# GpSimd's casts, squares and gathers wait for the VectorE instruction ahead of them, in a new order of all queues

## The chip, the cores and the metric

One Trainium2 chip, one of its cores. The metric is the time of one execution on the device in microseconds (us); the time of a kernel is the median of its runs.

## The reference

Block-sparse attention, and on its result a feed-forward network (FFN) with a squared relu:

```python
# q, k, v: (4, 8, 768, 64) f32; blocks of 32 rows, 24 of them; sampled_blocks: (24, 3)
scores = q @ k.T / 8
mask   = |blk_i - blk_j| <= 1  or blk_i in (0, 23)  or blk_j in (0, 23)  or blk_j in sampled_blocks[blk_i]
attn   = softmax(where(mask, scores, -1e9))
x      = (attn @ v), heads side by side           # 3072 x 512
out    = relu(x @ w_in) ** 2 @ w_out              # 512 -> 2048 -> 512
```

## The kernel before

Work is cut into tasks of a few instructions each. A task is a Python function with the things it waits for and the buffers that it takes and frees. One string, `PROGRAM`, lists all tasks in the order in which they are emitted: a word `V48` is task 48 on VectorE (DVE), `P` is TensorE (PE), `A` ScalarE (ACT), `G` GpSimd (POOL), `S` SyncE (SP, the queue of most DMAs), and `/2` says which of the four PSUM tiles `X` the task takes. Each engine executes its own words in order and waits by semaphores only for what a task depends on. So the string sets both the order on each queue and, for work that several engines can do, the engine.

A unit `u` is two heads of one batch (16 units, 4 per batch). Loads bring q, k, v in f32; `cast_qk` and `cast_v` turn them into bf16 (in `qc` and `VB`) on DVE, POOL or ACT; q and k are transposed into `QKT` on PE (batch 0, `transp`, `evac`) or by a DMA of SP (`transp_dma`).

Batches 0 and 1 are done densely, 256 queries at a time: `scores` on PE, `exps` on ACT (line 360, into a `pT` buffer), `masks` on DVE (line 367: `pT` times a mask tile that lies in a `VG` buffer), `values` on PE, `normalize` on DVE (lines 410 and 413), and a transposition into the FFN's input `xT`.

Batches 2 and 3 are done in six visits `v` of 128 queries (two groups `g` of two blocks). For a group only the needed keys and values are brought together: `k_gather` (lines 593 to 599) copies keys from `QKT` to a `KG` buffer with block numbers from registers, on POOL or DVE. `v_gather` brings rows of V from a copy in HBM to a `VG` buffer, either by one indirect DMA from POOL (line 579) or by six DMAs from SP with block numbers from registers (line 582); `v_window` brings the rows that need no number (lines 552, 556). Then `s_scores`, `s_exps` (623), `s_masks` on DVE (630), `s_values` (653), `s_normalize` on DVE (659, 662, into `XS`) and `s_transp`, a transposing DMA of SP from `XS` into `xT` (666). The registers are filled by `load_blocks` (TENSOR_LOAD, line 561) from the table `tab`.

The FFN takes tiles of 256 rows: `hidden` on PE (four parts for each of four units of 512 hidden columns), `relu` on ACT (707) or DVE (709), `square` on ACT (718), POOL or DVE (720), `output` on PE, `out_copy` on ACT or DVE (121, 123), `store`. `w_load` brings the weights in eight parts on POOL's queue. Line 203 is the helper `pair`, which issues nearly all matmuls; 121 and 123 are the helper `copy`.

Of the kernel before, what the change touches and what calls it, by code (L numbers as in the profile page):

```python
# [17 lines left out]
AOP = mybir.AluOpType  # L18

P = 128  # L20
# [5 lines left out]
def kernel(  # L26
# [92 lines left out]
    def copy(e, out, in_):  # L119
        if e == "ACT":  # L120
            A.copy(out=out, in_=in_)
        else:
            (V if e == "DVE" else G).tensor_copy(out=out, in_=in_)  # L123
# [239 lines left out]
    def masks(a, e):  # L363
        u, q0, w, cs = a
        pT = ptile[a].rearrange("p h (c q) -> p h c q", q=w)
        m = MK[q0][:, cs[0]:cs[-1] + 1]
        V.tensor_tensor(out=pT, in0=pT, in1=m[:, None].broadcast_to([P, 2, len(cs), w]), op=AOP.mult)  # L367
# [216 lines left out]
    def k_gather(b, v, g, e):  # L584
# [8 lines left out]
        eng.tensor_copy(out=to[:, :, 0], in_=src[:, :, :, 2 * w * (g - 1):2 * w * (g + 1)])  # L593
        if there.get((n, g % 2)) != b:
            there[n, g % 2] = b
            eng.tensor_copy(out=rows[:, :, :, RS * w:(RS + 1) * w], in_=src[:, :, :, 0:w])
            eng.tensor_copy(out=rows[:, :, :, (RS + 1) * w:], in_=src[:, :, :, (nb - 1) * w:nb * w])
        for r_ in range(RS):
            eng.tensor_copy(out=rows[:, :, :, r_ * w:(r_ + 1) * w], in_=src[:, :, :, bass.ds(at[r_] * w, w)])  # L599
# [26 lines left out]
    def s_masks(u, v, gs, e):  # L626
# [3 lines left out]
        V.tensor_tensor(out=pT, in0=pT, in1=m[:, None].broadcast_to([P, 2, n]), op=AOP.mult)  # L630
# [82 lines left out]
    def square(T, f, i, n, e):  # L713
# [5 lines left out]
        else:  # L719
            (G if e == "POOL" else V).tensor_mul(out=g, in0=r, in1=r)  # L720
# [217 lines left out]
    tb["slots"] = T_(table_slots, deps=[t, p], get=tmp)  # L938
    hb = Buf("X")
# [26 lines left out]
    for T in TILES:  # L966
# [3 lines left out]
        for f in range(0, NF, n_u):  # L970
# [4 lines left out]
            for part in range(parts):  # L975
# [4 lines left out]
                             put=[xb[b, c0]] if f + n_u == NF and end else []))  # L980
# [21 lines left out]
        A29 G35 P4/3 V32 P30/0 P12/2 P14/3 P9/1 P5/1 V31 P33/1 V111 P36/3 P0/2 A37 V1 V34 P102/2 V209 V46 P47/0 P106/1 A103 V48 P104/3  # L1002
        V43 A107 P44/0 G57 P7/2 V45 A105 P58/1 V54 P113/0 V59 P55/2 A114 P117/3 G41 V56 P2/1 V67 A118 P115/2 V3 P108/0 A116 V64 P127/1
        V109 P10/3 P65/3 A128 P123/2 V66 A124 P68/1 P125/3 G75 V69 V63 P92/1 P110 A126 P133/2 G76 V112 A134 P137/3 G52 S28 S42 S18 S19
        V93 S20 P88/0 A138 G38 V155 V89 P84/1 P119/2 G74 V85 A60 P86/0 P39/3 P135/1 V120 G73 A87 V40 A136 P121 P61/0 G49 P129/3 V122
        V62 G77 V70 P176/2 P170/0 P139/1 A177 G81 V130 G80 A171 V140 P146/2 P131 V132 A147 P149/3 V172 P71/0 P141 V142 A150 V72 P50/2
        P173/1 V148 P781/0 A174 P782 V178 P189/3 P783 V51 A190 V175 P90/1 P15/2 P96/2 P784 V91 A97 P183/3 V151 A785 P94/2 P179/1 V95
        A184 G787 P143/0 P774/2 V180 P775 A144 V191 G78 P186/3 P181 P776 V182 A187 P777 V145 P157/0 V778 A786 P152/3 A158 P160/1 V188
        P788/2 A161 V153 P163/0 P789 V185 A164 P790 V162 P154 P217/1 P791 A156 V159 A218 P192/0 V165 P795/3 A792 V193 S82 P166/1 S83
        V296 V219 S53 S254 A779 G794 S253 P194 P100/2 A780 P796 V195 V167 A101 P214/0 P797 G793 A215 P168 P798 V169 P211/2 V799 P824/1  # L1010
        G79 A212 P825 P196/0 G256 V216 P826 A197 P199/3 P818/2 G801 S257 P827 A200 P819 V828 P202/0 A800 S261 P228/3 P820 G22 A203
        S262 P821 V213 P812/1 S269 A229 V822 P813 G258 P220/0 A829 P814 V201 P245/2 S259 P221 A246 V198 P815 P802/3 V222 A816 P231/2
        V266 P223 P803 A232 V204 S267 P239/1 V230 P804 A224 A240 V264 S270 P242/0 P205/2 V233 S265 A243 P225/1 P206 P805 V207 A226
        S277 V274 P288/0 S436 S255 P208 P806 V227 A289 S275 V247 P11/1 P291/1 A823 P234/0 V241 P807 A292 V210 V244 P98/2 P235 V272
        P808 A99 V236 A817 S273 P298/2 V290 P248/1 P237 A299 P809 V238 S278 V293 P285/0 S279 V300 P249 A810 P830/2 V250 P831 A286 V282
        P304/3 P251 P832 V260 A305 P301/0 V252 P833 S263 V287 P852/1 A302 S334 S283 V834 P853 P846/3 G280 P313/0 V303 P854 A314 P316/2
        S281 P855 P847 A317 V856 G284 P294/0 P848 A835 S271 P295 V306 P310/1 S21 P849 G268 V297 A311 P864/2 V318 P865 S440 A850 P307/0
        V315 P866 S438 A857 P308 G851 S446 P355/3 P867 V309 A356 P322/1 V868 P858/0 P859 A323 P349/3 V357 P325/2 P860 A350 V312 P861
        P836/1 V276 A326 V351 S456 P319/3 A862 P328/2 V327 S439 P320 S447 A329 V321 P352/0 P837 S811 V324 A353 S454 P339/2 V330 P838
        A340 V354 P331/3 P342/0 A869 S385 V341 P332 P358/2 V333 P839 A343 V23 S335 G441 P359 A863 P336/3 P361/0 G443 P840 A337 P841  # L1020
        G451 A362 S622 P364/3 G449 P842 A365 P373/0 G445 S450 P843 A374 G461 P870/3 A844 S444 P367/0 V338 P871 A368 V344 S463 P872
        V347 V360 S455 V366 S442 P376/0 P345/1 A377 V363 P379/2 P346 P873 S452 V348 A380 V369 P403/0 P874 A404 V375 S464 P370/2 V378
        P400/1 P393/0 V381 P371 A401 P875 V372 S471 S448 A394 V402 P382/1 P390/2 V405 P383 A391 P387/0 P876 V384 A388 V395 S386 P406/1
        P886/2 V392 A407 P887 V457 P427/0 P877 A428 V465 P24/1 P888 S497 S462 A878 G453 P889 V408 S458 P880/0 A890 P881 P430/3 S466
        P882 V27 G891 A431 P883 P409/2 A884 P926/3 V26 P927 A885 P410 G469 P415/0 V398 V25 P928 V411 G467 A416 P892/1 S608 V389 P424/2
        S879 P893 A425 P929 S468 V432 P894 A930 P895 V426 P396/0 S470 A896 P16/2 V429 P898/3 S845 P397 S616 A931 P418/2 P433/1 V399
        P899 V459 A419 P932/0 P933 V474 S460 P412/2 P900 A413 P901 V417 P934 A902 S473 P434 V420 P935 V435 P482/3 G903 P904/2 A483
        V936 A897 P492/1 P905 V414 A493 P914/3 G503 P915 P480/0 S499 S623 P421/1 A481 P916 S542 P422 P906 G472 V423 V484 P907 S437
        G937 P917 P487/1 P908 V918 A488 P477/1 P490/0 P909 G501 A478 V504 A491 P485/1 P920/3 A919 G543 V494 P921 V479 V621 P475/0 P910
        A486 G500 V489 V625 A476 P911 V613 P495/1 A912 G546 S632 S913 V547 P511/2 S607 P505/0 V496 P922 A512 S520 S502 P923 A506  # L1030
        P954/1 V924 G627 P955 P514/2 P508/0 P956 A515 V507 G524 P557/3 S545 P957 V513 A509 P948/2 A925 P949 S614 P938/0 G544 A558 S498
        P939 V516 A958 V525 P551/3 S523 P950 A552 P940 V510 P554/3 P951 A555 P548/1 P941 G589 S628 A549 P517/3 A952 P966/1 G959 V518
        A953 P967 P535/2 P942 V550 S519 A536 P529/3 P943 G521 S626 V559 P526/2 P944 V590 G522 A527 P945 V537 P968 V609 A946 P960/2
        P961 V556 A530 P969 V528 P532/0 P962 A970 S540 S615 V553 P963 S585 G586 S624 P988/3 A971 V964 P989 P560/1 A533 V531 P990 A965
        V534 P594/2 P994/0 V561 A595 P995 P991 G567 S562 P996 A992 P538/1 V619 V568 S631 A993 P597/3 P972/2 S606 V539 A598 P997 V596
        S541 P600/1 P973 A601 G587 P1000/3 A998 V617 S620 P974 G999 P975 S610 P572/1 P1001 A573 S630 P982/0 G637 P1002 S588 P1003
        P575/1 P983 V1004 A576 P976 V611 P984 P578/1 P569/3 P985 V629 S612 A570 P977 V599 A986 V633 P978 S563 G565 S618 A579 V602
        P1034/3 A1005 P591/0 G635 V574 S634 P979 A592 P1035 G564 S638 P1028/1 A980 V593 P1036 S566 V580 P1029 A987 P1037 P1030 S639
# [50 lines left out]
```

## Time and profile before

| | before |
|---|---|
| times of 3 runs | 257.20, 259.04, 257.91 us |
| median | 257.91 us |
| the profiled execution | 258.88 us |
| its span in the profile | 257.10 us |
| granted TensorE clock | 1.00 |
| PE, DVE, ACT, POOL busy | 243.1, 171.3, 183.6, 98.8 us |

The span goes from the first to the last recorded instruction or transfer; 1.78 us of the profiled execution lie outside it. Busy times are sums over one engine, and PEld (weight loads) overlaps PE. In the lines of the trace, `X<-xT,w_in_sb` reads: output X, inputs xT and w_in_sb; what stands in brackets behind a line is the time that the engine stood idle before it and what ended that wait.

### The profile page before, as it was taken

To read this page: it belongs to the slowest core of one execution; us is meant where nothing else is said; L and a number is where in the kernel's file an instruction comes from. 1 tells how busy PE (TensorE), PEld (TensorE's weight loads), DVE (VectorE), ACT (ScalarE), POOL (GpSimd) and SP (SyncE) were. 2 spreads that over 40 slices of the span, in tenths; PEclk is the share of its full clock that TensorE was granted. 3 is DMA by queue.
4 is the path that set the end of the run, shared out by engine and by line. 5 is a ranking of instruction groups with operands and counts; after the bars stand their busy time and mean duration, and the time that the engine had idled before them with its cause. 6 is when DMAs were issued, how large, how long until landed. Compare 5 with 4: busy or idle time off the path is not lost.

```text
span 257.1 us, 12061 instructions
## 1 busy us (share of the span) xinstructions
PE 243.1 (95%) x5265; PEld 182.1 (71%) x5265; DVE 171.3 (67%) x408; ACT 183.6 (71%) x217; POOL 98.8 (38%) x178
## 2 busy tenths in 40 slices
PE   7888999999999997998998999999999999999993
PEld 4667879678874677975864867866875677767683
DVE  7778988899889995969916756657536725730301
ACT  3899999998999797846783975675965286623640
POOL 3183247003316026198556314264357620412100
PEclk9999999999999999999999999999999999999999
DMA  6999989999999996999699779998474923044022
GB/s 200 374 250 207 206 205 155 270 202 252 250 281 179 197 202 153 340 229 154 188 243 202 194 174 167 251 214 199 129 206 95 189 40 60 5 121 148 23 86 83
DMA packets 64692, 47.08 MB, mean 183 GB/s; under 512 B 31567, under 2 KB 60624, under 8 KB 64640
## 3 DMA queue, kind: packets, MB, share of 16 engines
q1 hardware_dynamic: 58512, 37.82, 64.7%
q0 software_dynamic: 5440, 8.05, 16.8%
q8 instruction: 41, 0.67, 1.1%
q10 hardware_dynamic: 688, 0.46, 0.6%
q14 instruction: 11, 0.09, 0.1%
HBM read 35.51 MB, written 7.91 MB: 169 GB/s over the span
## 4 chain that ended last, share of the span: by engine, by line
PE 53%; DVE 5%; DVEq 1%; issue 1%; ACT 1%; ACTq 0%
PE X L203 49%; PE X L653 4%; DVE VB L123 1%; ACT pT L623 1%; DVEq L561 1%; DVE MKS L123 1%; DVE pT L630 1%; DVE r L709 0%; DVE KG L599 0%; DVE qc L123 0%; DVE XS L413 0%; DVE KG L593 0%; DVE XS L662 0%; DVEq L599 0%; DVE rs L410 0%
## 5 line engine op out<-in xcount | busy, mean ns | idle before, releaser
L203 PE MATMUL X<-xT,w_in_sb 64*128 64x256 bf16 x1536 | 100.8, 269 | 2.8 <-issue 1.5
L203 PE MATMUL X<-w_out_sb,g 64*128 64x512 bf16 (+3 forms) x960 | 95.2, 334 | 0.1
L203 PEld LDWEIGHTS <-w_in_sb 64*128 64x128 bf16 x1536 | 74.6, 94 | 16.0 <-issue 5.4
L360 ACT ACTIVATE pT<-X 128x1024 bf16<-128x1024 f32 x72 | 70.6, 1030 | 7.6 <-PE X L203 6.8
L623 ACT ACTIVATE pT<-X 128x768 bf16<-128x768 f32 (+1 forms) x56 | 41.6, 766 | 26.5 <-PE X L203 23.9
L203 PEld LDWEIGHTS <-g 64*128 64x128 bf16 x960 | 40.3, 94 | 26.3 <-PE X L203 0.4
L720 POOL TENSOR_TENSOR g<-r 128x1024 bf16<-128x1024 f32 (+1 forms) x20 | 31.6, 1587 | 64.4 <-ACT r L707 47.2
L707 ACT ACTIVATE r<-X 128x1024 f32<-128x1024 f32 x28 | 29.8, 1068 | 20.6 <-PE X L203 20.5
L709 DVE TENSOR_SCALAR r<-X 128x1024 f32<-128x1024 f32 x20 | 24.5, 1224 | 26.7 <-PE X L203 13.7
L367 DVE TENSOR_TENSOR pT<-pT,VG 128x1024 bf16<-128x1024 bf16 x60 | 40.9, 715 | 0.2
L718 ACT ACTIVATE g<-r 128x1024 bf16<-128x1024 f32 (+1 forms) x40 | 35.2, 899 | 2.7 <-DVE r L709 2.5
L203 PE MATMUL X<-QKT 64*128 64x256 bf16 (+1 forms) x384 | 31.6, 250 | 3.3 <-DVE XS L413 1.3
L630 DVE TENSOR_TENSOR pT<-pT,MKS 128x768 bf16<-128x768 bf16 (+1 forms) x48 | 27.6, 607 | 10.7 <-ACT pT L623 10.5
L203 PEld LDWEIGHTS <-QKT 64*128 64x128 bf16 x384 | 16.7, 95 | 9.5 <-issue 4.1
L579 POOL DMA_INDIRECT VG<-rows,idx x19 | 20.2, 1061 | 4.4 <-issue 2.6
L203 PEld LDWEIGHTS <-pT 64*128 64x128 bf16 x768 | 16.0, 94 | 1.9
L203 PE MATMUL X<-VB,pT 64*128 64x65 bf16 x768 | 17.1, 190 | 0.0
L203 PEld LDWEIGHTS <-KG 64*128 64x128 bf16 x528 | 13.8, 95 | 4.5 <-issue 0.2
L659 DVE RECIPROCAL ss<-X 128x8 f32<-128x8 f32 x12 | 2.5, 206 | 19.5 <-PE X L653 17.3
L653 PEld LDWEIGHTS <-pT 128*64 128x64 bf16 x624 | 11.9, 111 | 4.9 <-issue 3.7
L203 PE MATMUL X<-QKT,KG 64*128 64x64 bf16 x528 | 15.3, 190 | 0.1
L123 POOL CAST VB<-vs 128x768 bf16<-128x768 f32 x9 | 7.8, 869 | 16.5 <-DMA vs<-in_v_dram 16.4
(107 smaller groups left out, 210.3 us busy)
## 6 DMA issues: line engine op xcount, KB each, us to landing
vs<-in_v_dram SPq DMA_DIRECT2D x14, 384.0 KB
ks<-in_k_dram SPq DMA_DIRECT2D x13, 384.0 KB
qs<-in_q_dram SPq DMA_DIRECT2D x12, 384.0 KB
out_dram<-ys SPq DMA_DIRECT2D x9, 512.0 KB
VG<-rows SPq DMA_DIRECT2D x20, 132.0 KB
w_in_sb<-in_moe_w_in_dram POOLq DMA_DIRECT2D x4, 512.0 KB, 8.6
w_out_sb<-in_moe_w_out_dram POOLq DMA_DIRECT2D x4, 512.0 KB, 9.9
rows<-VB SPq DMA_DIRECT2D x2, 792.0 KB
```

Source lines behind the costliest of these rows:

```text
L123: (V if e == "DVE" else G).tensor_copy(out=out, in_=in_)
L203: last = nc.tensor.matmul(out(r ^ crossed), lhsT(r ^ crossed, rows), rhs(r ^ crossed, rows), skip_group_check=True, **kw)
L360: A.activation(out=pT[:, :, 0:n], in_=stile.pop(a)[:, :, 0:n], func=AF.Exp, scale=scale)
L367: V.tensor_tensor(out=pT, in0=pT, in1=m[:, None].broadcast_to([P, 2, len(cs), w]), op=AOP.mult)
L579: G.indirect_dma_start(out=to[0:RS * HB], out_offset=None, in_=pairs, in_offset=bass.IndirectOffsetOnAxis(ap=idx[0:RS * HB, g - 1:g], axis=0))
L623: A.activation(out=pT[:, :, 0:n], in_=stile.pop((u, v, gs))[:, :, 0:n], func=AF.Exp, scale=scale)
L630: V.tensor_tensor(out=pT, in0=pT, in1=m[:, None].broadcast_to([P, 2, n]), op=AOP.mult)
L653: nc.tensor.matmul(po[i * D:(i + 1) * D, h, a * VW:(a + 1) * VW], pts[g][:, h, c * D:(c + 1) * D], val, start=a == 0 and c == 0, stop=c == ...
L707: A.activation(out=to, in_=src, func=AF.Relu)
L709: V.tensor_scalar(out=to, in0=src, scalar1=0.0, scalar2=None, op0=AOP.max)
L718: A.activation(out=g, in_=r, func=AF.Square)
L720: (G if e == "POOL" else V).tensor_mul(out=g, in0=r, in1=r)
```

## The change

It has four parts.

1. A new helper, `through_port`, is put around the masks (`masks`, `s_masks`), the casts of q, k and v, the copies of `k_gather` and the squares. On DVE it remembers the instruction. On POOL it makes the instruction wait for the one of DVE that was remembered last, if no other POOL instruction has waited for it yet. DVE does not wait for POOL in return. 39 tasks of POOL carry such a wait in the new order.
2. `load_blocks` is no longer a part of `table_rows`. It becomes six tasks of its own: for POOL, DVE and SP, one for the groups below 4 and one for the others.
3. The last part of `hidden` of each unit, not only of the tile's last unit, counts as a user of the `xT` buffer, so that units may come in any order.
4. `PROGRAM` is new: another order on all queues, and other engines for some tasks. DVE has fewer casts (11 fewer of 128x384 keys, for instance), three more output copies (2 to 5) and two more relus (20 to 22). ACT has three fewer output copies (9 to 6), two fewer relus, and three more half squares (15 to 18). POOL has more casts, 6 instead of 9 half squares, and 11 instead of 19 indirect gathers. The eight others are six DMAs each on SP: its `v_gather` DMAs go from 18 to 66. The number of matmuls, 5265, stays.

```diff
     def copy(e, out, in_):
         if e == "ACT":
-            A.copy(out=out, in_=in_)
-        else:
-            (V if e == "DVE" else G).tensor_copy(out=out, in_=in_)
+            return A.copy(out=out, in_=in_)
+        return (V if e == "DVE" else G).tensor_copy(out=out, in_=in_)
+
+    before_port = []
+
+    def through_port(e, made):
+        if e == "DVE":
+            before_port[:] = [made.ins]
+        elif e == "POOL" and before_port:
+            tc.add_manual_dep(made.ins, before_port.pop().name, SYNC, reason="the port that both read through")
...
-        copy(e, VB[b % 2][:, :, 2 * a:2 * a + 2, 0:D].rearrange("p n t d -> p t n d"), raw[u][2])
+        through_port(e, copy(e, VB[b % 2][:, :, 2 * a:2 * a + 2, 0:D].rearrange("p n t d -> p t n d"), raw[u][2]))
...
-        V.tensor_tensor(out=pT, in0=pT, in1=m[:, None].broadcast_to([P, 2, n]), op=AOP.mult)
+        through_port(e, V.tensor_tensor(out=pT, in0=pT, in1=m[:, None].broadcast_to([P, 2, n]), op=AOP.mult))
...
-            (G if e == "POOL" else V).tensor_mul(out=g, in0=r, in1=r)
+            through_port(e, (G if e == "POOL" else V).tensor_mul(out=g, in0=r, in1=r))
...
     def table_rows(e):
         V.tensor_scalar(out=idx, in0=low[1][:, P:P + GR], scalar1=float(HB), scalar2=lane, op0=AOP.mult, op1=AOP.add)
-        load_blocks("POOL")
-        load_blocks("DVE")
-        load_blocks("SP")
...
-    def load_blocks(e):
-        for g in wanted[e]:
+    def load_blocks(g0, g1, e):
+        for g in [g_ for g_ in wanted[e] if g0 <= g_ < g1]:
...
+    for e_ in ("POOL", "DVE", "SP"):
+        T_(load_blocks, 0, 4, deps=[tb["slots"]])
+        T_(load_blocks, 4, nb, deps=[tb["slots"]])
...
-                             put=[xb[b, c0]] if f + n_u == NF and end else []))
+                             put=[xb[b, c0]] if end else []))
...
-        A29 G35 P4/3 V32 P30/0 P12/2 P14/3 P9/1 P5/1 V31 P33/1 V111 P36/3 P0/2 A37 V1 V34 P102/2 V209 V46 P47/0 P106/1 A103 V48 P104/3
+        P0/0 P17/1 A35 A302 V117 A18 A38 G41 P36/2 V1 P2/3 S161 P39/1 G52 G60 P14/0 G63 G47 P34 V3 P92/3 P42/0 A37 P94/2 A93 V40 G58
```

In the new kernel the lines stand some four to seven further down: the masks at 374 and 634, the gathers of V at 583 and 586, the squares at 724.

POOL's queue before, at the middle of the program (batch 2's first visits). `L579` are indirect gathers of V, `L720` is a square; the brackets name the semaphores that an instruction waits for.

```order
L579 DMA VG_207<-rows_70,idx 96x1056 [waits DMAHW5_49,DMASW0_49,DVE_49]
L720 TENSOR_TENSOR g_99<-r_82 128x1024 [waits DVE_49]
L579 DMA VG_208<-rows_70,idx 96x1056 [waits DMASW1_49]
L579 DMA VG_209<-rows_70,idx 96x1056 [waits DMASW2_49]
L579 DMA VG_208<-rows_70,idx 96x1056 [waits DMASW3_49,DVE_49]
L593 COPY KG_118<-QKT 128x4x64 [waits PE_49]
```

And in the new order, at the same visits:

```order
L583 DMA VG_208<-rows_70,idx 96x1056 [waits DMASW2_49]
L122 CAST VB_191<-vs_79 128x2x6x64 [waits DVE_49]
L122 CAST qc_106<-ks_77 128x384 [waits DMAHW0_49,DMAHW3_49,DVE_49,Pool_49]
L122 CAST qc_106<-ks_77 128x384 [waits Pool_49]
L724 TENSOR_TENSOR g_100<-r_83 128x1024 [waits Activation_49]
L724 TENSOR_TENSOR g_101<-r_81 128x1024 [waits DVE_49,Activation_49]
L597 COPY KG_119<-QKT 128x4x64 [waits PE_49,Pool_49]
```

Casts for batch 3 stand here now in place of gathers; the casts and the second square wait for DVE.

DVE's queue before, where the tables for the visits are finished, among the last masks of batch 1. `MKS` are the masks of the visits, `idx` the rows that the indirect gathers take.

```order
L367 TENSOR_TENSOR pT_87<-pT_87,VG_208 128x1024
L123 CAST MKS<-X_147 128x5x64 x3
L123 CAST MKS<-X_147 128x6x64 x3
L524 TENSOR_SCALAR idx<-X_147,lane 128x11
L561 TENSOR_LOAD tab x6
L410 RECIPROCAL rs<-X_148 128x4
L413 TENSOR_TENSOR XS<-X_148,rs 128x2x2x64
```

The new order has the loads at two places, ahead of the first gather of keys on DVE and, further down, ahead of the division of batch 2's first visit (`ss`):

```order
L417 RECIPROCAL rs<-X_147 128x4
L420 TENSOR_TENSOR XS<-X_147,rs 128x2x2x64
L565 TENSOR_LOAD tab x2
L597 COPY KG_118<-QKT 128x4x64
...
L634 TENSOR_TENSOR pT_87<-pT_87,MKS 128x2x192
L565 TENSOR_LOAD tab x4
L663 RECIPROCAL ss<-X_148 128x8
L666 TENSOR_TENSOR XS<-X_148,ss 128x2x4x64
```

Two loads instead of six stand in front of a gather, and four between a mask and a division.

SP's queue in the new order, where batch 2's later visits are prepared. `L670` is the transposition of a finished visit into `xT`, `L586` a row gather of V with its register arithmetic (`ISA`).

```order
L560 DMA VG_207<-rows_70 64x2x528 x2
L156 DMA vs_79<-in_v_dram 128x2x384
L158 DMA qs_74<-in_q_dram 128x6x128
L319 DMA_TRANSPOSE QKT<-qc_106 128x6x128
L670 DMA_TRANSPOSE xT_117<-XS 128x4x128
L586 ISA
L586 DMA VG_209<-rows_70 16x1056
```

The last pair of rows comes six times for one gather. Before, this stretch of SP's queue held windows of V (`L552`, `L556`), loads and transpositions only.

More of the change, by code (lines that the diff above doesn't have):

```diff
@@ L290, in cast_qk @@
             for i in range(2):
-                copy(e, c[:, 3 * i:3 * i + 3], raw[u][w].rearrange("p t (m e) d -> p e m t d", e=2)[:, i])
+                through_port(e, copy(e, c[:, 3 * i:3 * i + 3], raw[u][w].rearrange("p t (m e) d -> p e m t d", e=2)[:, i]))
         else:
-            copy(e, c, raw[u][w].rearrange("p t n d -> p n t d")[:, ns])
+            through_port(e, copy(e, c, raw[u][w].rearrange("p t n d -> p n t d")[:, ns]))
         cast[u, w, ns.start] = c
@@ L366, in masks @@
         m = MK[q0][:, cs[0]:cs[-1] + 1]
-        V.tensor_tensor(out=pT, in0=pT, in1=m[:, None].broadcast_to([P, 2, len(cs), w]), op=AOP.mult)
+        through_port(e, V.tensor_tensor(out=pT, in0=pT, in1=m[:, None].broadcast_to([P, 2, len(cs), w]), op=AOP.mult))
     def outs_of(t, w):
@@ L592, in k_gather @@
         rows = to[:, :, 1:3].rearrange("p a z e j -> p a z (e j)")
-        eng.tensor_copy(out=to[:, :, 0], in_=src[:, :, :, 2 * w * (g - 1):2 * w * (g + 1)])
+        through_port(e, eng.tensor_copy(out=to[:, :, 0], in_=src[:, :, :, 2 * w * (g - 1):2 * w * (g + 1)]))
         if there.get((n, g % 2)) != b:
             there[n, g % 2] = b
-            eng.tensor_copy(out=rows[:, :, :, RS * w:(RS + 1) * w], in_=src[:, :, :, 0:w])
-            eng.tensor_copy(out=rows[:, :, :, (RS + 1) * w:], in_=src[:, :, :, (nb - 1) * w:nb * w])
+            through_port(e, eng.tensor_copy(out=rows[:, :, :, RS * w:(RS + 1) * w], in_=src[:, :, :, 0:w]))
+            through_port(e, eng.tensor_copy(out=rows[:, :, :, (RS + 1) * w:], in_=src[:, :, :, (nb - 1) * w:nb * w]))
         for r_ in range(RS):
-            eng.tensor_copy(out=rows[:, :, :, r_ * w:(r_ + 1) * w], in_=src[:, :, :, bass.ds(at[r_] * w, w)])
+            through_port(e, eng.tensor_copy(out=rows[:, :, :, r_ * w:(r_ + 1) * w], in_=src[:, :, :, bass.ds(at[r_] * w, w)]))
     def s_scores(u, v, gs, buf, e):
@@ L1006 @@
[L1006 to L1017, printed above, removed]
@@ L1054 @@
[L1054 to L1056 removed]
+        P0/0 P17/1 A35 A302 V117 A18 A38 G41 P36/2 V1 P2/3 S161 P39/1 G52 G60 P14/0 G63 G47 P34 V3 P92/3 P42/0 A37 P94/2 A93 V40 G58
+        G81 P53/1 P90/3 V43 G80 V49 P112/0 G19 A54 P108/1 A113 P98/0 A91 P50/3 A109 V95 P110/2 G82 V51 A99 P61/1 P121/3 P64/0 A111 V73
@@ new lines @@
+        S715 S736 S760 S1055 A750 S738 P752/1 A753 P1084 P1098 P743/2 P1085 P765/1 P1099 P1086 V1100 A766 P1087 A744 P771/1 A772
+        P1102/2 P1124/0 V1088 P1103 P774/1 P1125 P1104 A775 P1126 P1105 S762 P768/3 A1106 V754 P1114/1 P1127 A769 G1101 A1107 V776
+        P1145/2 P1146 P1115 A1128 P1147 V745 P1116 G1129 A1130 V751 V767 V770 P746/3 P1131/0 P1132 A747 V773 S761 P1148 P1133 P1134
+        V748 P755/3 V1149 V756 A1135 A1137 S758 G1151 P777/2 V778 P1138/0 P1139 S779 P1117 P1152/3 P1118 P1140 A1136 P1141 P1119 P1120
@@ L1057 @@
+        V1208 S1209 P11/2 S1219
     """
```

90 lines of the change are left out of this document (48 added, 42 removed).

## Prediction

> **What bounds the kernel now.** First the page, for what is busy and what the chain that ended last consists of; then three windows, for where TensorE (PE) is idle; then the waits, for who stands idle for whom.
>
> ```profile
> PE 243.1 (95%) x5265; PEld 182.1 (71%) x5265; DVE 171.3 (67%) x408; ACT 183.6 (71%) x217; POOL 98.8 (38%) x178
> PE 53%; DVE 5%; DVEq 1%; issue 1%; ACT 1%; ACTq 0%
> ```
>
> PE works 243.1 us of a span of 257.1 and holds most of the chain. The change takes no matmul away, so what can be won lies in the 14.0 us in which PE is idle. The windows say where those are.
>
> ```profile
> 0.00:30.00 30.00, 25.32 (x496) 19.46 (x496) 23.98 (x64) 24.31 (x28) 12.47 (x28) 1.00 1.05 250
> 30.00:250.00 220.00, 214.57 (x4609) 159.63 (x4607) 146.56 (x343) 158.98 (x189) 86.34 (x150) 1.00 0.82 177
> 250.00:257.10 7.10, 3.22 (x168) 2.98 (x165) 0.72 (x2) 0.27 (x1) 0.00 (x0) 1.00 0.23 76
> ```
>
> After the window and its length come PE, PEld, DVE, ACT and POOL, then the granted clock, which is 1.00 throughout. PE is idle 4.7 us in the first 30, 5.4 us in the 220 us of the middle, and 3.9 us at the end. The other engines have slack in the middle: DVE 73 us, ACT 61, POOL 134.
>
> ```profile
> POOL g L720 <- ACT r L707: 47.2, 9, 7.8
> DVE ss L659 <- PE X L653: 17.3, 8, 5.1
> PEld L203 <- issue: 10.6, 25, 1.2
> PE X L203 <- DVE XS L413: 1.3, 2, 1.0
> ```
>
> Read: GpSimd stood 47.2 us before squares whose relu ScalarE had not done; DVE stood 17.3 us before normalizations for PE. PE's own waits for an engine are small. The largest in the middle is 1.0 us (last row), and many small ones are "issue", in which PE waits for nothing that the profile shows. So no single wait sets the time.
>
> **Part 1: the wait of GpSimd for the mask ahead of it.** What it is aimed at is in the timeline (start, length, operation):
>
> ```profile
> 113.89 1.90 POOL L720 TENSOR_TENSOR g<-r 128x1024 bf16<-128x1024 f32 x1
> 114.06 1.97 DVE L630 TENSOR_TENSOR pT<-pT,MKS 128x384 bf16<-128x384 bf16 x1
> 119.10 0.35 DVE L630 TENSOR_TENSOR pT<-pT,MKS 128x384 bf16<-128x384 bf16 x1
> 217.97 2.71 DVE L630 TENSOR_TENSOR pT<-pT,MKS 128x768 bf16<-128x768 bf16 x2
> 218.13 2.13 POOL L720 TENSOR_TENSOR g<-r 128x1024 bf16<-128x1024 f32 x1 [7.74 <-DVE r L709]
> 221.16 1.03 DVE L630 TENSOR_TENSOR pT<-pT,MKS 128x768 bf16<-128x768 bf16 x2 [0.48 <-ACT pT L623]
> ```
>
> A mask of 0.35 us took 1.97 when a square on GpSimd had begun 0.17 us before it; it ended at 116.03, the square at 115.79. Two masks that take 1.03 us together took 2.71 around the square at 218.13. How much of this there is in all comes from the groups, each mean against a clean row of the same shape:
>
> ```profile
> L367 DVE TENSOR_TENSOR pT<-pT,VG 128x1024 bf16<-128x1024 bf16 x60 | 40.9, 715 | 0.2
> 52.74 0.68 DVE L367 TENSOR_TENSOR pT<-pT,VG 128x1024 bf16<-128x1024 bf16 x1
> L630 DVE TENSOR_TENSOR pT<-pT,MKS 128x768 bf16<-128x768 bf16 x40 | 23.3, 613 | 10.7 <-ACT pT L623 10.5
> L630 DVE TENSOR_TENSOR pT<-pT,MKS 128x384 bf16<-128x384 bf16 x8 | 4.4, 577 | 0.0
> L123 DVE CAST VB<-vs 128x768 bf16<-128x768 f32 x5 | 4.8, 967 | 0.0
> 118.63 0.55 DVE L123 CAST VB<-vs 128x768 bf16<-128x768 f32 x1
> ```
>
> 60 x (715 - 680) ns is 2.1 us; 40 x (613 - 515) is 3.9; 8 x (577 - 350) is 1.8; 5 x (967 - 550) is 2.1: **9.9 us of DVE time** is lost beside GpSimd. That is much on DVE and little on PE. Around the costliest place PE waited here:
>
> ```profile
> 118.75 0.30 PE L203 MATMUL X<-xT,w_in_sb 64*128 64x256 bf16 x2 [0.36 <-issue]
> ```
>
> Between 30 and 250 us PE is idle 5.4 us altogether, and at 118 to 120 us, with DVE on the chain, the row names issue. So all collisions together can cost PE nothing at least and 5.4 us at most; I take 0.5, near the lower end, since that row is the one beside the worst collisions and names no DVE. In the new order 39 steps on GpSimd carry the wait. Behind a held square stand casts and gathers; they have 134 us of slack in the middle, and the 47.2 us row shows that squares on GpSimd already come late without harm to PE. Two waits in a row, as in the rows of GpSimd's queue shown above (cast of V, square g_101), hold it about as long as the masks last: 0.35 to 0.68 us each. **-0.5**, bounds -5.4 and +1.4 (39 waits at 0.35 us is 13.7 us on GpSimd; a tenth of that reaching PE).
>
> By the Trainium skill ("SBUF — State Buffer", section "SBUF: two separate sides") the port pair that DVE and GpSimd share is an exclusive lock: whichever starts first keeps it for its whole instruction. The trace agrees at 114.06, where the mask ended 0.24 us after the square; by that rule the wait alone frees nothing where another mask follows: part 1 would be 0 and the sum below -1.0. The kernel's own rows for this are in the first rival.
>
> **Part 2: the register loads of block numbers.** Before, DVE loads six groups in a row, with the division of a normalization behind them:
>
> ```profile
> L561 DVEq TENSOR_LOAD <-tab x6: 857/992/1067, 93.8 to 99.2; - x6
> 100.21 0.18 DVE L410 RECIPROCAL rs<-X 128x4 f32<-128x4 f32 x1 [2.66 <-ACT pT L360]
> 100.91 0.39 PE L203 MATMUL X<-QKT 64*128 64x256 bf16 x4 [1.02 <-DVE XS L413]
> ```
>
> Six by 0.99 us end at 100.2; normalization follows and PE waits 1.02 us for it. This wait goes: **-1.0**. New are two loads before the first gather of keys and four between a mask and the normalization of batch 2's first visit. Four are 4.0 us on DVE in the worst place; the loads begin as soon as that mask ends, while PE still has the visit's values and other tiles' FFN work to do. Their price on PE lies between 0 and 3 us; nearest is the old case, where six loads (5.95 us) cost PE 1.0, so four by that ratio **+0.7**. Sum of the part -0.3. Late next is the transposition after that normalization.
>
> **Part 3: work that changes engine.** The rows of the groups that change most:
>
> ```profile
> L123 DVE CAST qc<-ks 128x384 bf16<-128x384 f32 x13 | 6.5, 545 | 0.2 <-DMA ks<-in_k_dram 0.2
> L123 DVE CAST qc<-ks 128x768 bf16<-128x768 f32 x3 | 1.7, 560 | 1.2 <-DMA ks<-in_k_dram 1.2
> L123 POOL CAST qc<-ks 128x384 bf16<-128x384 f32 x4 | 1.9, 513 | 8.4 <-DVE ids L486 8.4
> L123 DVE COPY ys<-X 128x1024 f32<-128x1024 f32 x2 | 2.4, 1222 | 0.1
> L709 DVE TENSOR_SCALAR r<-X 128x1024 f32<-128x1024 f32 x20 | 24.5, 1224 | 26.7 <-PE X L203 13.7 <-POOL g L720 10.2 <-POOL KG L599 1.6
> L707 ACT ACTIVATE r<-X 128x1024 f32<-128x1024 f32 x28 | 29.8, 1068 | 20.6 <-PE X L203 20.5
> L718 ACT ACTIVATE g<-r 128x512 bf16<-128x512 f32 x15 | 8.8, 626 | 2.6 <-DVE r L709 2.5
> L121 ACT COPY ys<-X 128x1024 f32<-128x1024 f32 x9 | 9.1, 1011 | 2.6 <-DMA out_dram<-ys 2.0 <-PE X L203 0.3
> ```
>
> DVE gives up 11 casts of half a key tile (11 x 0.545 = 6.0 us), two whole ones (1.1), three of values (3 x 0.967 = 2.9) and five of queries at about 0.55 (2.7): 12.7 us. It takes three output copies (3.7) and two relus (2.4): **DVE about 6.6 us lighter**. ACT gives up three output copies (3.0) and two relus (2.1) and takes three half squares (1.9) and one more mask tile (about 1): 2 us lighter. GpSimd takes ten of the key casts (10 x 0.513 = 5.1) and some ten others of 0.5 to 0.9, and gives up eight indirect gathers (8.5, row below) and three half squares: about 3 us heavier. On engines 67 to 71% busy, 9 us less is worth little to PE. The price lies between nothing (all of it was slack) and 5.4 us (all idle of the middle); nearest is the first, by the 73 and 61 us of slack. I take **-1.0**, in which the earlier casts and transpositions of units 4 to 7 are contained.
>
> **Part 4: eight gathers of V go from GpSimd to SP.** Each becomes six transfers, 48 in all:
>
> ```profile
> L579 POOL DMA_INDIRECT VG<-rows,idx x19 | 20.2, 1061 | 4.4 <-issue 2.6 <-PE X L203 0.9 <-DVE pT L630 0.3
> 190.46 3.35 SPq L582 DMA_DIRECT2D VG<-rows  x6
> 174.25 2.51 SPq L666 DMA_TRANSPOSE xT<-XS  x2
> 180.64 13.85 PE X L203 x284
> ```
>
> 3.35 us for six is 0.56 each: 48 are 26.8 us on SP's queue, for 8.5 us less on GpSimd. SP is off the chain, but the transpositions that hidden waits for stand in the same queue. The one pair above leaves SP at 176.76, and PE begins that run of FFN work at 180.64: 3.9 us of cover. One gather (3.35) ahead of a transposition fits, two (6.7) do not if they fall due then. Most are due earlier, when a buffer comes free one or two visits ahead. **+0.5**, bounds 0 and 6 (third rival).
>
> **Part 5: head and end.** In the first 30 us the idle 4.7 us stands beside a DMA share of 1.05 and ACT busy for 24.3 of 30 (first of the three windows); the new order brings the mask rows first and loads the second weight part before the first. Nothing in the trace prices that; its bounds are the idle itself on one side (-2, about half) and as much on the other: **0**. The end:
>
> ```profile
> 253.40 0.29 DVE L123 COPY qs<-X 128x128 f32<-128x128 f32 x1 [1.97 <-PE X L203]
> 253.72 0.37 ACTq L776 DMA_DIRECT2D out_dram<-qs  x1
> ```
>
> After the last matmul come one copy (0.29), one issue (0.37) and the landing: 3.8 us. The same sized last piece leaves on the same queue in the new order; the output before it is 128x256 instead of 128x128 on SP: **0**, bounds -0.5 and +0.5. The early release of the xT buffer costs no instruction.
>
> **Sum.** -0.5 - 0.3 - 1.0 + 0.5 + 0 = -1.3, rounded to **-1.5** for the many small issue gaps that a new order shuffles. The profiled execution took 258.88 us (span 257.10 and 1.78 around it), 0.97 above the median of 257.91. So a like execution would take about 257.4, and the median **256.4 us**, 0.6% less. Within 1% (some 2.6 us) a measurement of this kernel can't tell a change from none.
>
> **Rivals.**
> *Collisions only move* (0.12, 257.9). The wait runs one way: it keeps GpSimd from starting before the mask that stands ahead of it, and the next mask can still run into the GpSimd work. The row at 218.13 is that case: the square began after the first of two masks and the second was held to its end. For it: masks come in runs (the rows with x2, 0.5 us each), and a square lasts 1.9 to 2.1. Against: the searched order may put squares where no mask follows. Then part 1 gives 0 and the order as much as it takes. The same time comes if the new waits decide nothing, because GpSimd waited for a relu longer anyway (the 47.2 us).
>
> *The order is better by more than its parts* (0.38, 253.3). Half of the idle time of the middle goes (2.7) and 1.9 of the 4.7 of the head: 4.6 less than 257.9. For it: all 14 us of idle time are made of small gaps that depend on the order, and both loaded engines become lighter. Against: 5.4 us in 220 is little, and a part of it is issue.
>
> *SP's queue becomes the bound* (0.22 with the four loads in a bad place, 260 to 262.5). In the new queue three gathers stand ahead of the transposition of batch 3's first visit: 18 x 0.56 = 10.0 us. If SP reaches the first of them less than 6.2 us before the normalized tile is there, the transposition is late by up to 10.0 - 3.9 = 6.1: 256.4 + 6.1 = 262.5. Half of it gives 259.5; at a second place three gathers stand ahead of batch 3's last two transpositions. For it: FFN work of that tile can't begin without it. Against: from 176.8 to 180.6 PE had other work, and buffers of gathered rows come free earlier than the tile is due.
>
> **How the numbers follow.** My forecast has 0.28 (its own range is 255.3 to 259.0), with the first rival 0.40 for within 1%; faster by over 1% 0.38; slower by over 1% 0.22. From below, 0.1 is left out under 251.0 (7 us of 14 gone), from above 0.1 over 261.5.
>
> **What would show it.** Mask rows near their clean lengths (L630 128x384 at 0.35 to 0.45, L367 at 0.68) with GpSimd's squares waiting for DVE show part 1; PE idle in 30 to 250 near 4 us shows the sum. A PE wait of over 1 us for XS of batch 2's first visit shows part 2 wrong; a wait of PE for DMA into xT shows the third rival; clean masks with the same PE idle show that the collisions never reached PE. The forecast falls if PE's idle time in the head moves by over 2 us, which no row here prices.

## The result: 268.25 us, 4% slower

The changed kernel takes 268.25 us (median of 4 runs, 266.23 to 268.37) against 257.56 us for the kernel before (4 runs). The ratio is 1.0398, 95% interval 1.0318 to 1.0477. The prediction was 256.4 us, 0.6% less, with a range up to 261.5. Times are medians of all runs of a kernel and ratios leave out its slow runs (over 1.5% above its fastest), so a ratio need not be the quotient of two medians. The page of the changed kernel, its three windows as before, and the waits in which PE, DVE or GpSimd stands idle for a transfer of gathered rows or of a transposition:

```profile
PE 245.2 (92%) x5265; PEld 182.2 (68%) x5265; DVE 166.2 (62%) x391; ACT 182.1 (68%) x215; POOL 102.6 (39%) x189
PE 70%; DMA 9%; DVE 7%; ACT 5%; SPq 4%; issue 2%; POOL 0%; DVEq 0%; POOLq 0%; ACTq 0%
```

```profile
0.00:30.00 30.00, 26.44 (x466) 20.32 (x468) 20.79 (x56) 24.21 (x30) 12.08 (x28) 1.00 1.05 253
30.00:250.00 220.00, 206.03 (x4479) 151.84 (x4477) 141.45 (x332) 154.28 (x180) 87.43 (x158) 0.99 0.80 174
250.00:266.40 16.40, 12.70 (x328) 10.05 (x323) 3.92 (x5) 3.61 (x6) 3.12 (x3) 0.99 0.21 75
```

```profile
PE X L657 <- DMA VG<-rows: 6.8, 2, 4.1
PE X L210 <- DMA xT<-XS: 3.9, 3, 1.6
PEld L657 <- DMA VG<-rows: 2.8, 1, 2.8
POOL g L724 <- DMA VG<-rows: 2.4, 1, 2.4
```

Two new things stand on the page: DMA (9%) and SP's queue (SPq, 4%) are now on the chain that ended last. PE's idle time went from 14.0 to 21.2 us: 1.1 less in the first 30 us, 8.5 more in the middle, 0.2 less at the end. PE's own busy time grew by 2.1 us. Together that is the 9.3 us by which the span grew (257.10 to 266.40). The 1.1 us of the head are no gain: PE was busy longer there because its matmuls ran slower in this execution. The same group of matmuls, nearly all in the head, in the kernel before, in this execution and in another one of the changed kernel (the one run beside the last experiments):

```profile
L203 PE MATMUL X<-R,oh 64*128 64x256 bf16 x66 | 8.0, 269 | 0.1
L210 PE MATMUL X<-R,oh 64*128 64x256 bf16 x66 | 10.6, 325 | 1.5 <-ACT pT L367 0.6 <-DVE R L122 0.5 <-ACT VG L284 0.3
L210 PE MATMUL X<-R,oh 64*128 64x256 bf16 x66 | 8.3, 270 | 2.1 <-ACT pT L367 1.1 <-DVE R L122 0.5 <-ACT VG L284 0.5
0.00:30.00 30.00, 24.54 (x475) 19.22 (x477) 21.89 (x58) 25.04 (x31) 11.92 (x28) 1.00 1.05 250
```

In that other execution (last line) PE idles 5.5 us in the head, 0.8 more than before, and PE is busy 243.4 us in all; its middle idles 8.2 us more than before, as here 8.5. So the loss sits in the middle. In the waits, two of PE for gathered rows of V (`VG<-rows`) make 6.8 us, three for a transposition (`xT<-XS`) 3.9; the page before had neither among PE's longest. The longest one, in the timeline of SP's queue (SPq) and of the visit's values (L657):

```profile
127.04 4.68 SPq L586 DMA_DIRECT2D VG<-rows  x6
...
134.84 2.45 SPq L319 DMA_TRANSPOSE QKT<-qc  x1
137.38 2.04 SPq L670 DMA_TRANSPOSE xT<-XS  x1
139.62 3.41 SPq L586 DMA_DIRECT2D VG<-rows  x6
142.57 0.25 PE L657 MATMUL X<-VG,pT 128*64 128x65 bf16 x3
146.96 1.45 PE L657 MATMUL X<-VG,pT 128*64 128x65 bf16 x45 [4.14 <-DMA VG<-rows]
```

The second gather (six transfers, 3.41 us) stands behind two transpositions that take SP 4.5 us. It has left SP at 143.0, PE began the visit's values at 142.6 and stood from 142.8 to 147.0 for the rows. Nearly all of that stand is the landing of the last of the six (4.12 us on the chain that ended last, where these transfers land in 2.2 us in the median). In that stretch the granted clock fell too:

```profile
140.00:150.00 10.00, 4.77 (x96) 3.19 (x94) 1.44 (x3) 2.76 (x4) 2.58 (x5) 0.83 1.03 173
```

PE idles 5.2 us there, at a mean clock of 0.83; the last section shows what that adds.

### The profile page after: what moved, and what is told of

Its sections match the earlier page's. It is cut to its first block, busy times and chain, and to the rows that moved or that the text cites. A ratio compares the mean times of both kernels' runs of the same rounds, so it can differ in the third digit from the quotient of the medians.

```text
span 266.4 us, 12256 instructions
## 1 busy us (share of the span) xinstructions
PE 245.2 (92%) x5265; PEld 182.2 (68%) x5265; DVE 166.2 (62%) x391; ACT 182.1 (68%) x215; POOL 102.6 (39%) x189
## 4 chain that ended last, share of the span: by engine, by line
PE 70%; DMA 9%; DVE 7%; ACT 5%; SPq 4%; issue 2%; POOL 0%; DVEq 0%; POOLq 0%; ACTq 0%
PE X L210 63%; DMA xT<-XS 4%; PE X L657 4%; ACT pT L367 3%; DVE pT L374 3%; SPq L586 2%; DMA QKT<-qc 2%; DMA VG<-rows 2%; PE X L405 2%; DVE r L713 1%; SPq L447 1%; PE X L312 1%; ACT r L711 1%; DVE pT L634 1%; SPq L560 1%
## 5 line engine op out<-in xcount | busy, mean ns | idle before, releaser
L374 DVE TENSOR_TENSOR pT<-pT,VG 128x1024 bf16<-128x1024 bf16 x60 | 44.3, 770 | 1.7 <-ACT pT L367 1.5
L711 ACT ACTIVATE r<-X 128x1024 f32<-128x1024 f32 x26 | 27.9, 1072 | 24.7 <-PE X L210 22.7
L724 POOL TENSOR_TENSOR g<-r 128x1024 bf16<-128x1024 f32 (+1 forms) x17 | 27.1, 1594 | 44.5 <-DVE r L713 18.8
L722 ACT ACTIVATE g<-r 128x1024 bf16<-128x1024 f32 (+1 forms) x43 | 37.2, 879 | 9.3 <-DVE r L713 8.8
L713 DVE TENSOR_SCALAR r<-X 128x1024 f32<-128x1024 f32 x22 | 26.8, 1222 | 18.5 <-PE X L210 17.6
L634 DVE TENSOR_TENSOR pT<-pT,MKS 128x768 bf16<-128x768 bf16 (+1 forms) x48 | 24.8, 555 | 12.9 <-ACT pT L627 12.9
L122 POOL CAST qc<-qs 128x384 bf16<-128x384 f32 (+3 forms) x21 | 12.6, 614 | 37.2 <-DVE pT L374 13.8
L657 PE MATMUL X<-VG,pT 128*64 128x65 bf16 x528 | 13.5, 201 | 6.8 <-DMA VG<-rows 6.8
L122 POOL CAST qc<-ks 128x384 bf16<-128x384 f32 (+1 forms) x18 | 11.4, 656 | 21.6 <-PE X L405 15.8
L657 PEld LDWEIGHTS <-pT 128*64 128x64 bf16 x624 | 12.4, 114 | 9.7 <-issue 6.8
L122 POOL CAST VB<-vs 128x768 bf16<-128x768 f32 x13 | 12.8, 986 | 11.8 <-DVE pT L374 4.4
```

The source lines that it names most:

```text
L122: return (V if e == "DVE" else G).tensor_copy(out=out, in_=in_)
L374: through_port(e, V.tensor_tensor(out=pT, in0=pT, in1=m[:, None].broadcast_to([P, 2, len(cs), w]), op=AOP.mult))
L634: through_port(e, V.tensor_tensor(out=pT, in0=pT, in1=m[:, None].broadcast_to([P, 2, n]), op=AOP.mult))
L657: nc.tensor.matmul(po[i * D:(i + 1) * D, h, a * VW:(a + 1) * VW], pts[g][:, h, c * D:(c + 1) * D], val, start=a == 0 and c == 0, stop=c == ...
L711: A.activation(out=to, in_=src, func=AF.Relu)
L713: V.tensor_scalar(out=to, in0=src, scalar1=0.0, scalar2=None, op0=AOP.max)
```

## The experiments

Theory one: the eight V gathers that went from GpSimd to SP, 48 issues, fill SP's queue, and the gathers and transpositions in it come late. Theory two: the new waits hold GpSimd back. Theory three: the rest of the new order is worse. The experiments ran on two chips, each beside the kernel before, which took 261 to 262 us there (257.7 to 267.4 over its runs) against 257.56 us in the first result; so ratios are compared and not times.

### Each cause alone

```diff
 # gathers on GpSimd: eight words of the new order
-S507 S550 S592 S570 S674 S718 S675 S760
+G507 G550 G592 G570 G674 G718 G675 G760
```

> The changed kernel with eight of its eleven V gathers on SP given back to GpSimd, at the same places of the order; everything else, the waits too, stays. Theory one (SP's queue is the cause: 48 more gather issues of 0.5 to 0.8 us hold up the gathers and transpositions that PE waits for): the 4.1 us wait of PE for VG at 143 us and the one at 170 to 174 us go, PE idle falls from 21.2 us to about 13 to 15, time 258 to 262. Theory two (the waits of GpSimd for DVE are the cause): stays at 266 to 270, or longer, since GpSimd gets more work. Theory three (the order of everything else): stays within 2 us of 268.

Measured: 264.86 us, 1.0155 (1.0072 to 1.0238). PE's waits for `VG<-rows` are gone. Half to three fifths of the loss go with them, not all; PE's idle time falls from 21.2 to 18.3 us and not to the 13 to 15 expected. What is left, 1.0155 and clear of 1, speaks for a part of theory three: with these gathers on GpSimd the rest of the new order is slower than the old one.

```diff
 # no waits
-            tc.add_manual_dep(made.ins, before_port.pop().name, SYNC, reason="the port that both read through")
+            before_port.pop()
```

> The changed kernel without the added waits: GpSimd's casts, squares and gathers wait for their own data alone, order and engines as in the changed kernel. Theory one (SP's queue): 266 to 269, no change within 1%. Theory two (the waits hold GpSimd's casts back, and with them transpositions of q and k and loads): 258 to 262. On the collisions: DVE's time lost beside GpSimd (11.7 us in the changed kernel by rows over their clean length) grows by 2 us or more if the waits do what they are meant for, and stays within 2 us if collisions only move.

Measured: 269.61 us, 1.0359 (1.0255 to 1.0463): no change against the changed kernel. Theory two falls. The groups of masks and key copies, with the waits (changed kernel):

```profile
L374 DVE TENSOR_TENSOR pT<-pT,VG 128x1024 bf16<-128x1024 bf16 x60 | 44.3, 770 | 1.7 <-ACT pT L367 1.5
L597 DVE COPY KG<-QKT 128x256 int32<-128x256 int32 x12 | 7.7, 639 | 1.7 <-issue 1.7
L634 DVE TENSOR_TENSOR pT<-pT,MKS 128x384 bf16<-128x384 bf16 x8 | 2.8, 355 | 5.9 <-ACT pT L627 5.9
L603 DVE COPY KG<-QKT 128x64 int32 x72 | 9.8, 207 | 0.0
```

and without them:

```profile
L374 DVE TENSOR_TENSOR pT<-pT,VG 128x1024 bf16<-128x1024 bf16 x60 | 42.9, 744 | 2.1 <-ACT pT L367 1.6
L597 DVE COPY KG<-QKT 128x256 int32<-128x256 int32 x12 | 7.5, 624 | 4.2 <-DMA QKT<-qc 2.5 <-issue 1.7
L634 DVE TENSOR_TENSOR pT<-pT,MKS 128x384 bf16<-128x384 bf16 x8 | 3.1, 397 | 6.6 <-ACT pT L627 6.6
L603 DVE COPY KG<-QKT 128x64 int32 x72 | 12.4, 241 | 0.0
```

The large masks and the large key copies hardly change; the small key copies do. In all DVE is 169.5 us busy without the waits and 166.2 with them (163.7 in the other execution of the changed kernel). So in the new order too the waits take 3.3 to 5.8 us off DVE, more than the 2 us set as the mark, and no time is gained.

The waits alone in the old order (the helper and its calls as in the change, the order as before):

> The kernel before with the waits alone: its own order and engines, and each cast, square and gather copy of GpSimd waits for the last mask, cast or gather copy of DVE ahead of it in the order. Theory one: 257 to 259, no change within 1%, and the mask at 114 us back at 0.35 us since the square behind it waits, while the one at 218 us stays long or another takes its place. Theory two: 261 or more.

Measured: 262.75 us, 0.9973 (0.9904 to 1.0041): no change. The waits did what they are meant for, at 218 us too, where the square was expected to stay in the way:

```profile
PE 244.8 (94%) x5265; PEld 183.9 (70%) x5265; DVE 166.1 (64%) x408; ACT 183.1 (70%) x217; POOL 97.8 (38%) x178
L637 DVE TENSOR_TENSOR pT<-pT,MKS 128x384 bf16<-128x384 bf16 x8 | 2.7, 362 | 0.7 <-ACT pT L630 0.7
L122 DVE CAST VB<-vs 128x768 bf16<-128x768 f32 x5 | 2.8, 554 | 0.0
222.18 1.02 DVE L637 TENSOR_TENSOR pT<-pT,MKS 128x768 bf16<-128x768 bf16 x2
222.80 2.14 POOL L727 TENSOR_TENSOR g<-r 128x1024 bf16<-128x1024 f32 x1 [8.20 <-DVE pT L637]
```

The small masks are back from 577 to 362 ns, the casts of V from 967 to 554, and the square that ran into two masks at 218 us before begins after both have, which take 1.02 us together again (2.71 before). DVE is 5.2 us less busy at the same amount of work. No gain in time can be seen from it.

The same eight gathers on SP in the old order:

```diff
-G501 G544 G586 G564 G668 G669 G712 G754
+S501 S544 S586 S564 S668 S669 S712 S754
```

> The kernel before with the same eight V gathers moved from GpSimd to SP at their places in its own order. Theory one in its simple form (48 more issues on SP cost time wherever they stand): 263 to 268. Theory one with the place (they cost only where SP has other urgent work ahead or behind): 258 to 263. Theories two and three: 257 to 259.

Measured: 271.38 us, 1.0378 (1.0268 to 1.0488). The old order with nothing but these gathers moved loses as much as the whole change, as the simple form of theory one has it, by the same waits:

```profile
PE X L203 <- DMA xT<-XS: 6.1, 3, 3.0
PE X L653 <- DMA VG<-rows: 5.1, 2, 3.6
```

Both edits at once, the eight gathers back on GpSimd and no added waits:

> The changed kernel with eight V gathers back on GpSimd and without the added waits: what is left is the new order of everything else. If the waits are free also where SP's queue does not set the time: 1.010 to 1.020 times the kernel before, as with the gathers back and the waits kept (1.0155). If the waits are what is left of the loss: 0.995 to 1.005.

Measured: 265.81 us, 1.0175 (1.0024 to 1.0327), like the 1.0155 with the waits kept. The waits cost nothing that can be seen here either, and DVE is 167.2 us busy without them, 162.0 with them.

### Issues, bytes or place

Eight issues instead of 48, for the same bytes (the sampled rows are replaced by fixed ones):

```diff
-            for j, r in enumerate(held_at[e][g]):
-                sy.dma_start(out=to[j * HB:(j + 1) * HB], in_=pairs[bass.ds(r * HB, HB)])
+            ...
+                sy.dma_start(out=to[0:RS * HB], in_=pairs[0:RS * HB])
```

> The changed kernel, but each of the eight gathers that SP took over is one transfer of the same 96 rows' size instead of six of 16, so 8 issues instead of 48; it brings fixed rows, not the sampled ones. Same bytes, same places, same waits. If the issue time on SP is the cause (3.4 us for six): the loss falls to 1.010 to 1.018 times the kernel before, as with the gathers on GpSimd. If the cause is that a gather on SP stands behind transpositions that wait (the place in the queue, whatever its length): 1.030 to 1.040. If it is the bytes or the landing: 1.030 to 1.040 too.

Measured: 259.31 us, 0.9946 (0.9891 to 1.0001). The whole loss is gone, more than with the gathers on GpSimd. The gather that PE waited for is one issue now (L589), after the same two transpositions. SP reaches these 4.6 us earlier, since the gather ahead of them takes 0.60 us instead of 4.68:

```profile
130.24 2.57 SPq L319 DMA_TRANSPOSE QKT<-qc  x1
132.90 1.99 SPq L673 DMA_TRANSPOSE xT<-XS  x1
134.94 0.57 SPq L589 DMA_DIRECT2D VG<-rows  x1
```

96 issues instead of 48:

```diff
-                sy.dma_start(out=to[j * HB:(j + 1) * HB], in_=pairs[bass.ds(r * HB, HB)])
+                for k in range(0, HB, n_):    # n_: 8 rows in the eight gathers, 16 in the others
+                    sy.dma_start(out=to[j * HB + k:j * HB + k + n_], in_=pairs[bass.ds(r * HB + k, n_)])
```

> The changed kernel with each of the 48 transfers of the eight gathers split in two of half the rows: 96 issues, the same bytes and the same places. If the number of issues on SP's queue is the cause: each gather takes some 6 us instead of 3.4 on SP, and the time rises again by about what the first 48 cost, to 1.06 to 1.09 times the kernel before. If the place alone or the bytes are: 1.03 to 1.045, as the changed kernel.

Measured: 286.46 us, 1.102 (1.086 to 1.1181), more than expected. The same gather, and PE's waits for such rows (the values are L659 here):

```profile
140.92 6.65 SPq L588 DMA_DIRECT2D VG<-rows  x12
PE X L659 <- DMA VG<-rows: 15.1, 5, 7.7
```

So with the same bytes 8, 48 and 96 issues give 0.995, 1.03 to 1.04 and 1.10. It is the issues: one of 16 rows (3.41 us for six) takes SP as long as one of 96 (0.57 us). The rows of the eight single issues are fixed and lie side by side; what that alone saves, no run separates.

The changed kernel on the same chip as the 96 issues and the next two experiments:

> The changed kernel itself once more, beside the three others on the same chip: 1.03 to 1.045 times the kernel before.

Measured: 267.02 us, 1.0293 (1.0167 to 1.042).

Two gathers moved ahead in SP's queue:

```diff
-... S507 P546 ... P969 S550 A555 ... S592 A579 ... P609/3 S570 A576 ...
+... S507 S550 P546 ... P969 A555 ... S592 S570 A579 ... P609/3 A576 ...
```

> The changed kernel with two of its V gathers on SP moved ahead in SP's queue: the second half of batch 2's visit 3 from behind a transposition into xT that waits for DVE, to right behind the gather before it, and the first half of visit 4 from behind another such transposition and the store of batch 3's values. These are the two for which PE waits in the changed kernel (4.1 us at 143 us, 2.8 us at 170 to 174). If the loss is two gathers that stand in the wrong place: 1.005 to 1.02 times the kernel before, both waits gone. If SP's queue as a whole is too full: 1.025 to 1.045, and the wait moves to the transpositions that they now hold up.

Measured: 269.06 us, 1.0317 (1.023 to 1.0405): no gain. Both waits for rows are gone from PE, and these stand in their place:

```profile
PE X L210 <- DMA xT<-XS: 5.7, 2, 3.1
PE X L210 <- DVE XS L666: 3.4, 1, 3.4
DVE XS L666 <- DMA xT<-XS: 3.7, 1, 3.7
```

```profile
130.77 6.91 SPq L586 DMA_DIRECT2D VG<-rows  x12
140.78 3.42 SPq L319 DMA_TRANSPOSE QKT<-qc  x1
144.29 1.35 SPq L670 DMA_TRANSPOSE xT<-XS  x1
```

Two gathers in a row hold SP for 6.9 us, and the transposition into `xT` begins 13.5 us after the first of them did, instead of 10.3. DVE then waits for its `XS` buffer, and PE for DVE. For these two gathers the place only chose what PE waits for.

The same two on GpSimd (`G550`, `G570`):

> The changed kernel with the same two gathers on GpSimd at their places, the six others on SP as they are. If the loss is these two: 1.005 to 1.02 times the kernel before. If each of the eight costs the same: 1.030 (six eighths of 1.040).

Measured: 265.7 us, 1.0207 (1.011 to 1.0305): lower than the changed kernel's 1.0293, but the intervals overlap. Whether each gather costs the same stays open.

### Two edits of the kernel before

Register loads ahead of each first use instead of six in a row:

```diff
-        load_blocks("POOL")
-        load_blocks("DVE")
-        load_blocks("SP")
...
-        eng, at = G if e == "POOL" else V, held_at[e][g]
+        eng, at = G if e == "POOL" else V, blocks(e, g)    # loads the registers of g if they aren't held
```

> The kernel before with the register loads taken out of the row of six and put each right ahead of the first gather that uses it, on DVE, GpSimd and SP. The prediction held that the six in a row cost PE 1.0 us at 100 us: 0.994 to 0.998 times the kernel before, and the wait of PE for XS at 100.9 us is gone. If that wait is hidden or moves on: 0.998 to 1.002. If a single load ahead of each gather holds up DVE more: over 1.002.

Measured: 263.94 us, 1.0121 (1.0022 to 1.022): no gain, rather a loss. The wait of PE at 100.9 us is gone, as expected. Another for a normalized tile came at 114 us:

```profile
PE X L203 <- DVE XS L413: 2.8, 2, 2.5
109.30 0.29 DVE L590 COPY KG<-QKT 128x256 int32<-128x256 int32 x1 [1.72 <-issue]
110.32 3.19 DVE L367 TENSOR_TENSOR pT<-pT,VG 128x1024 bf16<-128x1024 bf16 x2
114.11 0.26 PE L203 MATMUL X<-QKT,KG 64*128 64x64 bf16 x6 [2.52 <-DVE XS L413]
```

DVE stands 1.72 us ahead of the copy, where the load is now, and two masks behind it take 3.19 us (1.29 in the kernel before, at 106.84), so the normalization behind them comes at 113.6 instead of 108.4.

No gather on SP:

```diff
-S690 S755 S732
+G690 G755 G732
```

> The kernel before with its three V gathers of SP given to GpSimd, so none is on SP. If each gather on SP costs the same (eight more cost 3.8%, so about 0.47% each): 0.985 to 0.990 times the kernel before. If a gather costs only where SP's queue is full, as at 120 to 180 us, and the three stand at 190 us and later, where PE idles for 0.2 us: 0.998 to 1.003.

Measured: 263.26 us, 1.0124 (1.0017 to 1.0231): no gain either. Its runs spread from 258.37 to 266.55 us, so a loss is not shown. Taking the last 18 issues off SP buys nothing where PE does not wait.

No version with all its work was faster than the kernel before by more than the noise.

## Why the prediction was wrong, point by point

**What bounds the kernel.** Right that only PE's idle time can move. Too narrow was the view that no single wait sets the time and so none would: the change made one. I also took DVE's, ACT's and GpSimd's slack from the windows and had no such row for SP, whose queue counts as no engine's busy time.

**Part 1, the waits (-0.5, bounds -5.4 and +1.4).** The size was near the truth, which is nothing: 0.9973 in the old order, and 1.0359 without them against 1.0293 and 1.0398 with them in the new one. In the old order they take 5.2 us off DVE. That the loss of DVE was off PE's path is shown by this. The rival "collisions only move" holds in part. Its own case, the square at 218, did not stay: with the waits the square came after both masks. But the new order brings more collisions: against the kernel before, its big masks went from 715 to 770 ns on average and its key copies from 349 to 639, with the waits or without them (744 and 624; 756 and 502 in the other execution of the changed kernel), while the small masks came to their clean length. One of these copies:

```profile
189.28 0.94 POOL L583 DMA_INDIRECT VG<-rows,idx  x1 [2.15 <-PE X L657]
190.05 2.25 DVE L597 COPY KG<-QKT 128x256 int32<-128x256 int32 x1
190.23 1.91 POOL L724 TENSOR_TENSOR g<-r 128x1024 bf16<-128x1024 f32 x1
```

The copy began 0.18 us ahead of the square and was held to its end (192.30 against 192.14; a copy of this shape takes 0.29 at 203.08). But GpSimd was at work already: its indirect gather ran from 189.28 to 190.22, over the start of the copy, and the square followed at once. By the Trainium skill ("SBUF — State Buffer", section "SBUF: two separate sides") the one that starts first keeps the ports for its whole instruction. This row does not speak against that, since a GpSimd instruction had started first; the mask at 114.06 in the kernel before agrees. Why the copy stayed held when the gather ended, no run shows.

**Part 2, register loads (-0.3).** The wait of 1.0 us for the old row of six is not among the waits of the changed kernel, and the four loads ahead of batch 2's normalization brought no wait of PE for it, so the +0.7 did not show. But that taking the row of six apart gains its 1.0 us was not confirmed: spread singly, the loads took that wait away and made the old order 1.2% slower, with a longer wait at the next place.

**Part 3, lighter engines (-1.0).** DVE came out 5.1 us lighter, ACT 1.5, GpSimd 3.8 heavier; 6.6, 2 and 3 were worked out. (The terms given for GpSimd add up to between -1.8 and +2.2 and not to 3.) Most of DVE's 5.1 came from the waits: without them it is 169.5 us, 1.8 lighter than before. That lighter engines gain 1.0 us is not shown. With eight single issues on SP the new order stands at 0.9946, 1.4 us under the kernel before (2.8 under to none), where the sum of all parts but the fourth is -1.8; but there GpSimd is free of the eight gathers as well, and the interval touches 1. With the gathers on GpSimd the same order is 1.55% slower than the kernel before, some 4 us.

**Part 4, the gathers on SP (+0.5, bounds 0 and 6).** This is the step that failed. The mechanism was in the text, as the third rival, at 0.22, and its sign came (PE waits 3.9 us for transpositions into `xT`); the size of the term was wrong. The move itself, eight gathers from GpSimd to SP, costs 3.78% in the old order, 9.7 us, and 1.4 to 2.4% in the new one (1.0155 to 1.0293 or 1.0398), 3.6 to 6.3 us: **4 to 10 us in place of 0.5**. In the new order 48 issues instead of eight cost 3.5 to 4.5%, 9 to 12 us. Two errors made it small. First, I asked only where a gather stands ahead of a transposition. PE's longest waits are the other way round: the gather stands behind transpositions that wait, and the values need it. The sentence that buffers come free one or two visits ahead was about when a gather may start, and not about when SP gets to it. Second, I set one cover of 3.9 us against one gather at a time. SP has one queue; what a late gather does not take from PE, the next transposition does (the two gathers moved ahead). The upper bound of 6 came from one place; in fact PE stood idle in five windows of 10 us between 100 and 210 us, 0.95 to 5.2 us in each.

**Part 5, head and end (0).** PE idled 1.1 us less in the head in one execution, in which its matmuls ran slower there, and 0.8 us more in the other; no gain is shown. The end gained 0.2. All lie within the bounds.

**What stays open.** With the gathers on GpSimd the new order is at 1.0155, with one issue each on SP at 0.9946. What the eight indirect gathers cost on GpSimd in these 2% (their time there, or the queue behind them) no run separates. GpSimd is 110.8 us busy with them and 102.6 in the changed kernel; but in both kernels with the gathers back PE's largest waits bear the name "issue" (2.2 and 3.4 us), in which the profile shows nothing that PE waits for.

## What to carry to other kernels

Work that is moved to an "idle" queue is priced by that queue's own timeline: add up what is issued there between the urgent entries, behind as well as ahead of them, before and after the move. A count of issues is a load like any other: here six transfers took the queue six times as long as one of the same bytes (3.41 us against 0.57). And time lost by an engine that PE does not wait for, here 5 us of DVE, is no gain when it is won back.

## What the runs showed of the hardware that was not expected

After the 4.1 us in which PE stood still in the changed kernel, its granted clock went down. By windows of 2 us:

```profile
144.00:146.00 2.00, 0.00 (x0) 0.00 (x0) 0.00 (x0) 0.00 (x0) 0.00 (x0) 1.00 1.04 165
146.00:148.00 2.00, 1.04 (x38) 1.07 (x40) 0.00 (x0) 0.00 (x0) 0.00 (x0) 0.63 1.10 282
148.00:150.00 2.00, 2.00 (x46) 1.33 (x42) 1.44 (x3) 0.80 (x2) 0.68 (x2) 0.51 0.97 114
150.00:152.00 2.00, 2.00 (x34) 0.94 (x28) 0.56 (x2) 2.00 (x4) 1.85 (x7) 1.00 0.78 204
```

It fell to about half for some 3.4 us (a mean of 0.83 over 10 us leaves 1.7 us of full clock out, and at half clock that is 3.4 us), up to 150 us. PE worked in the last 3.0 of these, from 146.96 on, so by estimate the half clock cost it 1.5 us and the wait 4.1 + 1.5. The 2.1 us by which PE was busy longer in the whole kernel can't be split in this way, since the slower head is in them too. The wait of 2.7 us at 172 us left the clock at 1.00. By the Trainium skill ("TensorE: Matmul & The Clock Gate", section "Part 1: The HAM clock gate (the "warmup" mystery)") the clock goes to half after an idle window of about 3.4 us and comes back after about as much work; this trace agrees. With 96 issues and 7.7 us idle in 10, the clock was lower over the window:

```profile
140.00:150.00 10.00, 2.35 (x53) 1.56 (x55) 0.00 (x0) 1.97 (x2) 1.90 (x3) 0.66 0.65 124
```

The prediction had no term for this: a wait of PE as long as this one costs more than its length. The slower matmuls of the head, 325 ns against 269 and 270, stand at a granted clock of 1.00 in the windows, so that column alone does not tell how fast they ran; why one execution had them and another of the same kernel did not, no run shows.
